# Fewer shift copies, an earlier first values product and split weight loads in a fused attention and MLP kernel

## The chip, the cores and the metric

The kernel runs on one core of a Trainium2 chip. The metric is the device time of one execution in microseconds. The version before takes 193.32 us (median of 6 runs, 193.03 to 193.96).

## The reference

The input x has 2048 positions of 448 values. Two blocks follow each other, each with a layer norm ahead of it and a residual around it.

```python
def _A_ref(x, wqkv, wo):            # 16 heads of 28
    qkv = x @ wqkv                  # -> q, k, v
    idx = pos[:, None] - 2 * arange(8)[None, :]        # 8 keys, two apart, masked where negative
    attn = softmax(where(mask, einsum(q, k[idx]) * scale, -1e9))
    return einsum(attn, v[idx]) @ wo

def _B_ref(x, w1, w2, w3, w4):      # F = 1792
    h = gelu(layernorm(x) @ w1)
    # four quarters of the 112 columns each, shifted by 1 down, 1 up, 2 down, 2 up along the positions
    hs = concatenate([g0, g1, g2, g3]) @ w2
    x1 = x + hs
    return x1 + gelu(layernorm(x1) @ w3) @ w4

h  = x + _A_ref(layernorm(x), A_wqkv, A_wo)
h2 = h + _B_ref(layernorm(h), B_w1, B_w2, B_w3, B_w4)
```

## The kernel before

**Chunks and tiles.** The 2048 positions are split into four chunks (c = 0 to 3) of 512. A chunk has four tiles of 128 positions. Its even positions are tiles 0 and 1 and its odd positions tiles 2 and 3, so that keys two positions apart stand side by side in one half. The 448 columns are laid out as four windows of 128 rows, which overlap, so that a matmul can use 64 rows of TensorE and two of them run at once.

**The stages of a chunk.** `phase_A1` computes the mean and variance of the four tiles, normalizes them into `lntm` and transposes them into `hT`. Chunks 0 and 1 are transposed by TensorE, with an evacuation from PSUM by `copy`, and chunks 2 and 3 by DMA. `phase_V` makes the values (`V_c`), five blocks of keys per half; `phase_QK` makes queries and keys (`QK_c.0` for heads 0 to 7, `QK_c.2` for heads 8 to 15). `phase_att` makes the scores of eight heads at a time (`S_c.g`, 80 small matmuls), the exponential on ScalarE, a mask on DVE, the products with the values (`AV_c.g`, 80 small matmuls) and the division by the sum (`N_c.g`). `phase_WO` is the output projection with the residual. `phase_B1` normalizes again, multiplies by w1 (`W1_c`), applies gelu, and makes the shifted copies (`G_c`). `phase_B2` multiplies by w2 (`W2_g`), `phase_W3` by w3 and `phase_B3` by w4 (`W4_g`). From w2 on the tiles are grouped anew, into groups of 2, 4, 4, 4 and 2 tiles, because a shift by two positions needs the neighbours' results.

**Quads.** `quad` (line 414) interleaves four products that go to two pairs of PSUM banks, T1 and T2. It makes four operations of TensorE: p1 and p2 start the products, p3 and p4 end those in T1 and T2. In `phase_V` p1 and p3 belong to the first two blocks of keys, which need only tiles 0 and 2, and p2 and p4 to the next two, which need all four tiles. A fifth product of values, `V_c.4`, follows.

**The first chunk.** `load0` issues the four tiles of x, then the weights: `win_load` (line 449) loads each of wqk and wv in two DMAs. `pad_wqk` (line 646) copies the query and key weights from `wqk_s` to `wqk_p` with 28 columns of a head padded to 32, by four copies of 128x896 elements (`pad`), and clears `wv_2`. For chunk 0 the square root is ScalarE's and the reciprocal DVE's (`inv_std_first`, line 565); later chunks take both from GpSimd.

**The shifts.** gelu of W1's second half goes to `gtm`. From there four copies of 32 partitions make `gB` and eight of 32 or 16 partitions make `gC`, each shifted by its own number of positions; in the last chunk three small memsets follow. `g_rows` (line 856) picks rows and offset for W2.

**What sets the order.** The code above only lists the operations and what each depends on. `_ORDER` (line 235) is a table of operation numbers, planned ahead of time: each engine executes its operations in the order of the table, a letter behind the number says which engine does a copy or a normalization (a: ScalarE, v: DVE, p: GpSimd), and the digits behind a colon name the PSUM banks. `_Sched.schedule` (line 159) reads it, `_emit_plan` (line 194) adds the waits. An engine never passes an operation that waits. The numbers `lat` and `occ` in the helpers served the planning and do nothing when the kernel runs. `WARM` is the number of TensorE's warm-up matmuls on zeros at the start, and `START` sets where TensorE's program begins within 256 instructions.

All instructions are recorded by one emitting line, so the profile has L1407 for all of them, and tiles and shapes tell them apart: `arena<-arena` is a pad, `ps<-arena,hT` values, `ps<-hT,arena` queries and keys, `ps<-qk` scores, `ps<-pt,vt` attention times values.

Of the kernel before, what the change touches and what calls it, by code (L numbers as in the profile page):

```python
# [228 lines left out]
WARM = 14  # L229
LATE = 2  # L230

START = 128
# [3 lines left out]
2 1 4 3 7 6 8 5 12 17 0 16 13 15 45 65 74 64 67 68 79 21 19 18:7 22 20 28 23 24 25 26 29 27 35 30 32 36:7 33:6  # L236
31 38 39:5 37a 41 34a 42:7 40v 43v 51:40 52 53 14 59 84 82 48v 156 47v 9 10 50a 62 63 80 49a 46a 78 69 134 132
72 73 138 136 135 139 133 137 11 178 142 54 180 85:62 71 86 87 88 184 205 185 140 182 70 179 98 99 101 103 102
113 109 111 110 106 107 104 112 108 105 57a 141 56a 97 89a 100 91:40 90a 92 220:26 93 201 181 143 221 223 144v
153v 150v 183 94 145:3 146a 147v 55:2 95a 96v 151:7 154:6 58v 148:3 152v 149v 203 76 75 77 222 224 188 155a  # L240
234:40 186 187 166:62 237 238 123p 167 168 204 60 235 236 61 225:54 198 165 115a 230 226 231 227 232 228 233 229
170a 169 171a 172:60 189 196a 173 174 175 197 239:54 161:3 240 244 241 245 242 246 243 247 66 130 190a 191 176a
177a 164a 346:06 382 192a 193 199 200 206 202 207 209 81 349 347 194v 157:42 158 159 117p 119v 160 348 208 162a
248:06 249 250 350 163a 360:24 252 251 361 254 253 210 213a 378:1 351:32 381a 363 362 255 356 260 364 256 121a
258 257 259 261 195 264 215a 389:60 352 390 214 118a 391 211a 217a 393a 262 365:54 370 366 371 367 372 368 369
218 263 392 394a 353 265 269v 267v 124 357 266a 383:26 354 535:04 538 373 536 219 384 385 386 355 388a 358 114p
268v 359 537 374:04 375 376 120v 387a 377 128 539 379a 116p 380a 528:26 416:04 529 417 270 418 531 419 540:6 530
216 532 126 420 421 403 424 122p 428 426 422 425 429 427 423 279:02 430 432 212 541a 543 125 431 280 281 282
533:6 283 534v 284 433 434v 437v 293a 294a 295a 439 436v 129 286v 288v 291v 292v 289v 440 404:04 435a 287a 405
406 407 296a 409a 542 408a 438 290a 273 271 272 274 544 441 395:62 396 397 398 285v 401v 400a 276v 278v 275v  # L250
277v 297:04 298 299 300 301 302 303 304 305 306 442 545 443a 549 446v 546 447:26 448 449 451 307 308 309 310 450
452 456v 459v 463v 454v 461a 457a 453v 462v 460a 458a 464a 445v 410:40 411 412 414a 455v 547 413 548 415v 131
312v 399:7 311v 402a 552 465:24 551 666:60 313 550 466 467 553 667 469 669 468 470 473 554:60 555 556 558 477
474 478 316:42 317 318 557 319 475 559 44 320 471 476 472 560 127 562 566 563 564 561 322:46 323 324 325 567 565
481 479 480 482 570 568 569 571 484v 579 483v 321 486v 328:02 577 578 314 329 330 331 327 326 334:46 335 670 332
336 333 668 338 337 485a 315 673:02 572v 340:5 487 339 343:7 676 574v 575a 573v 576 671:2 341 674 677 675 678:0
344 672v 489 490 492:64 493 494 488 495 491 680 679a 681 682 683 684 685 687 497 496 342 686 580 583v 585:02 586
587 588 589 590 599v 600a 595v 596v 592a 498:64 591v 594v 499 500 501 601a 593v 503 504:20 505 506 507 602a 597v
598v 581v 502 508 444v 603:64 604 605 607 83 609 611 509 610 688 510:02 511 512 513 689 612 606 608 691 613 514
615 690 616 614 515 617 516:7 519:6 692:42 693 694 695 517 520 618 518 619 620 623v 624v 621v 622a 625 627 521  # L260
697 696 704 698 700 701 699 705 702 703 706 707 708 525:7 744 522:6 629 745 526 523 709 713a 642:42 643 644 710v
712a 711v 524 714 717 626 527 645 584v 630:60 631 632 633 647 715 716 718 646 635 634 636:42 637 582v 638 640
746 639 641 723:60 724 725 648:24 649 650 727 652 726 728 722v 719v 732a 720v 736v 733v 735a 739v 730v 741a 734
731v 729v 742 738a 743a 740v 651 653 737 654:7 812:02 813 814 721v 815 655 816 817 820 345 818 821 819 749:64
750 751 752 824 753 754 757 656 755 758 822 823 825 756 759 761 762 760 765 747:3 628 663:2 763 764 660:7 826a
827a 828 664 766 748 661 662 770a 769v 768v 767v 657:6 849:24 850 851 852 771 658 831:60 832 833 854 853 835
837:24 834 836 838 839 840 843:06 844 845 842 841 829 846 848 830 847 782:24 783 784 788:06 786 785 787 789 790
791 792 793 665 776:42 777 778 780 794:60 795 796 797 779 781 799 858:5 659 774 806:4 855:3 859 856 857 860 798
772 775 800:7 807 773 801 802 808 803:6 809:7 804 805 810 811
# [3 lines left out]
def _fast_path(nc, es, flag, A_x, A_wqkv, A_wo, B_w1, B_w2, B_w3, B_w4, out):  # L273
# [33 lines left out]
    gB = sb("gB", [128, 2, HALF + 4], BF16)  # L307
    gC = sb("gC", [128, HALF + 4], BF16)
    gtm = sb("gtm", [128, 2, 768], BF16)
# [60 lines left out]
    def shift(out_ap, in_ap, n, on_pool=False):  # L370

        ka = dict(out=out_ap, in_=in_ap)
        op = S.add_many("flex", [("tensor_copy", ka)], 0, 0)
        op.opts = {"dve": [("tensor_copy", ka)], "pool": [("tensor_copy", ka)], "act": [("activation", dict(ka, func=ACT.Copy))]}
        op.lat = {"dve": dve_t(n, 3.0), "pool": 150 + n / 0.9, "act": 186 + n / 1.2}
        if not on_pool:
            del op.opts["pool"]
        op.occ = {e: v - {"dve": 82, "pool": 20, "act": 93}[e] for e, v in op.lat.items()}
        return op
# [34 lines left out]
    def quad(outs, lhsTs, rhss, n, T1, T2, blocks=(FIRST, SECOND) * 2):  # L414
# [20 lines left out]
        p1 = halves_op(series(0, 0, True), series(1, 1, True), g, mode)  # L435
        p2 = halves_op(series(2, 0, True), series(3, 1, True), (), mode)
# [12 lines left out]
    def win_load(name, dst, src, nbytes, engs):  # L449

        for k in range(2):
            dma("%s%d" % (name, k), dst[:, 2 * k:2 * k + 2, :],
                src[192 * k:192 * k + 256, :].rearrange("(c k) n -> k c n", k=128), nbytes / 2, engs[k],
                430.0)
# [4 lines left out]
    for il in range(4):  # L459
        dma("x0_%d" % il, xt(xin, 0, il, 1), x_rows(A_x, 0, il, 1), 128 * D * 2, ("sp", "act")[il % 2])  # L460
    win_load("wqk", wqk_s, A_wqkv[:, 0:2 * D], 512 * 2 * D * 2, ("sp", "sp"))
    win_load("wv", wv_s, A_wqkv[:, 2 * D:3 * D], 512 * D * 2, ("sp", "sp"))
# [17 lines left out]
    def init1():  # L480
# [28 lines left out]
        pool("memset", 140, ap=gB[:, :, 0:2], constant=0.0)  # L509
        pool("memset", 140, ap=gB[:, :, HALF:HALF + 2], constant=0.0)  # L510
        pool("memset", 140, ap=gC[:, 0:2], constant=0.0)

    def load_attn_out():
# [9 lines left out]
        for g in range(4):  # L523
            for h in range(2):
                k = 64 * h + 32 * (g // 2) + 16 * (1 - g % 2)
                dma("w2%d" % (3 + 2 * g + h), w2_s[k:k + 16, 3, :], w2v[96:112, g, :], 16 * D * 2)
# [4 lines left out]
        for x in range(2):  # L531
            for g, o in ((x, 384), (2 + x, 480), (2 + x, 544), (x, 576)):
                o += 16 * (1 - x)
# [31 lines left out]
    def inv_std_first(i0):  # L565
# [933 lines left out]
```

## Time and profile before

| | us |
|---|---|
| median of the runs | 193.32 |
| the profiled execution | 192.8 |
| its span | 191.1 |
| TensorE busy with matmuls | 182.9 |
| DVE busy | 128.8 |
| ScalarE busy | 112.2 |
| GpSimd busy | 41.2 |
| first matmul that isn't warm-up | 6.61 |
| last matmul ends | 188.24 |

The profile records one execution, whose own time stands beside its span; the difference lies before the first and behind the last instruction. PE is TensorE's matmuls, PEld its weight loads, DVE the vector engine, ACT ScalarE, POOL GpSimd, SP the engine that issues most DMAs. In a timeline the first number is the start in us, the second the duration, and a bracket gives the idle time ahead of it and what ended it; consecutive instructions of one kind are one line with a count. In the groups, busy time and mean duration in ns stand ahead of the second bar.

### The profile page before, as it was taken

How to read it: one execution, taken by the hardware profiler on the slowest of the kernel's cores; microseconds unless marked ns; L12 is line 12 of the kernel's file. 1: busy time of each engine (PE TensorE's matmuls, PEld its weight loads, DVE VectorE, ACT ScalarE, POOL GpSimd, SP SyncE). 2: the span in 40 equal slices, each digit the busy share in tenths (PEclk: the TensorE clock that was granted, in tenths of full speed). 3: DMA queues.
4: the chain of work that ended last, by engine and by line, in shares of the span. 5: the costliest groups of instructions: out<-in, count | busy, mean ns of one | idle time of the engine just before them, and what ended most of it. 6: DMA issues, size and time to landing. Idle time of an engine off the chain costs nothing.

```text
span 191.1 us, 6790 instructions
## 1 busy us (share of the span) xinstructions
PE 182.9 (96%) x2999; PEld 102.5 (54%) x2999; DVE 128.8 (67%) x313; ACT 112.2 (59%) x149; POOL 41.2 (22%) x101
## 2 busy tenths in 40 slices
PE   7899999997998998999999999999999999999994
PEld 2455556553556573577556464444566568455551
DVE  7799998999986689999773379894038970001241
ACT  2869899597849849938658920117691326554000
POOL 4137500607104603006900002042000320000000
PEclk9999999999999999999999999999999999999999
DMA  5965316427397766730643600507000233000031
GB/s 139 336 225 157 81 36 146 34 33 137 106 171 201 196 157 139 47 113 3 123 107 95 159 3 2 141 18 182 0 0 27 47 98 98 3 0 3 3 100 51
DMA packets 32479, 17.77 MB, mean 93 GB/s; under 512 B 22524, under 2 KB 31932, under 8 KB 32444
## 3 DMA queue, kind: packets, MB, share of 16 engines
q1 hardware_dynamic: 32156, 17.05, 38.5%
q8 instruction: 25, 0.41, 0.9%
q10 hardware_dynamic: 288, 0.23, 0.4%
q14 instruction: 10, 0.08, 0.2%
HBM read 10.07 MB, written 1.90 MB: 63 GB/s over the span
## 4 chain that ended last, share of the span: by engine, by line
PE 74%; DVE 10%; ACT 8%; DMA 3%; SPq 1%; issue 1%
PE ps L1407 74%; DVE st L1407 4%; DMA arena<-in_A_wqkv_dram 3%; ACT gC L1407 2%; DVE osb L1407 1%; ACT gtm L1407 1%; SPq L1407 1%; DVE xin L1407 1%; ACT gA L1407 1%; ACT pt L1407 1%; ACT vt L1407 1%; DVE arena L1407 1%; ACT arena L1407 1%; DVE lntm L1407 1%; DVE pt L1407 1%
## 5 line engine op out<-in xcount | busy, mean ns | idle before, releaser
L1407 PE MATMUL ps<-actT,w_s 64*128 64x512 bf16 (+2 forms) x560 | 44.2, 312 | 0.0
L1407 PE MATMUL ps<-w_s,arena 128*128 128x448 bf16 x224 | 43.4, 353 | 0.1
L1407 DVE TENSOR_TENSOR xb<-ps,xb 128x448 bf16<-128x448 f32 (+1 forms) x26 | 18.4, 723 | 32.8 <-PE ps L1407 32.7
L1407 ACT ACTIVATE arena<-ps 128x512 bf16<-128x512 f32 (+2 forms) x40 | 29.0, 767 | 16.9 <-PE ps L1407 16.6
L1407 PEld LDWEIGHTS ps<-actT,w_s 64*128 64x128 bf16 x560 | 26.4, 94 | 16.9 <-DVE xb L1407 0.4
L1407 PEld LDWEIGHTS ps<-w_s,arena 128*128 128x128 bf16 x224 | 21.4, 98 | 21.0 <-issue 0.6
L1407 PE MATMUL ps<-hT,arena 64*128 64x512 bf16 x224 | 25.9, 377 | 0.2
L1407 POOL TENSOR_TENSOR rstd<-vtmp,mhalf 128x4 f32<-128x4 f32 (+1 forms) x16 | 18.1, 1133 | 1.1
L1407 DVE BATCH_NORM_STATS2 st<-xin 128x6 f32<-128x448 bf16 x32 | 18.1, 604 | 0.2 <-DMA xin<-in_A_x_dram 0.2
L1407 ACT ACTIVATE pt<-ps 128x1024 bf16<-128x1024 f32 x16 | 15.7, 1022 | 3.7 <-PE ps L1407 3.6
L1407 PEld LDWEIGHTS ps<-hT,arena 64*128 64x128 bf16 x224 | 10.7, 94 | 11.9 <-ACT qk L1407 0.5
L1407 ACT ACTIVATE lntm<-xin,nmr,rstd 128x512 bf16<-128x512 bf16 x13 | 10.2, 808 | 9.0 <-POOL nmr L1407 8.3
L1407 PE MATMUL ps<-arena,hT 64*64 64x448 bf16 (+1 forms) x248 | 15.1, 352 | 0.2 <-DVE hT L1407 0.2
L1407 ACT ACTIVATE qk<-ps 128x1024 bf16<-128x1024 f32 x14 | 13.9, 1021 | 2.1 <-PE ps L1407 2.0
L1407 POOL TENSOR_SCALAR nmr<-mv 128x4 f32<-128x4 f32 (+1 forms) x16 | 5.1, 319 | 42.5 <-DVE mv L1407 42.3
L1407 POOL TENSOR_SCALAR vtmp<-mv 128x4 f32<-128x4 f32 (+1 forms) x16 | 3.4, 213 | 49.5 <-DVE mv L1407 48.6
L1407 PE MATMUL ps<-wo_s,oT 64*128 64x448 bf16 x128 | 13.1, 350 | 0.5 <-ACT vt L1407 0.5
L1407 PE MATMUL ps<-actT,w_p 64*128 64x512 bf16 (+1 forms) x140 | 13.0, 333 | 0.0
L1407 ACT ACTIVATE lntm<-xb,nmr,rstd 128x512 bf16<-128x512 bf16 x5 | 4.0, 811 | 15.1 <-POOL nmr L1407 15.1
L1407 DVE COPY gC<-gtm 32x256 bf16<-32x256 bf16 (+1 forms) x15 | 3.3, 220 | 13.6 <-ACT gtm L1407 13.2
L1407 DVE TENSOR_TENSOR pt<-pt,msk 128x1024 bf16<-128x1024 bf16 x16 | 10.5, 679 | 1.0 <-ACT pt L1407 1.0
L1407 PEld LDWEIGHTS ps<-arena,hT 64*64 64x64 bf16 (+1 forms) x248 | 7.6, 107 | 5.6 <-ACT gC L1407 0.8
(90 smaller groups left out, 226.5 us busy)
## 6 DMA issues: line engine op xcount, KB each, us to landing
w_s<-in_B_w_dram SPq DMA_DIRECT2D x6, 448.0 KB, 4.4
rzb<-rz_scratch SPq DMA_DIRECT2D x8, 256.0 KB, 4.6
out_dram<-xb SPq DMA_DIRECT2D x16, 112.0 KB, 2.2
xin<-in_A_x_dram SPq DMA_DIRECT2D x3, 448.0 KB, 7.3
arena<-in_A_wqkv_dram SPq DMA_DIRECT2D x2, 448.0 KB, 5.8
w_s<-in_B_w_dram SPq DMA_DIRECT2D x2, 336.0 KB, 5.1
arena<-in_A_wqkv_dram SPq DMA_DIRECT2D x2, 224.0 KB, 5.1
w_s<-in_B_w_dram SPq DMA_DIRECT2D x2, 224.0 KB, 2.9
```

The lines of the kernel that those rows point to most:

```text
L1407: inst = getattr(eng, meth)(**kw)
```

## The change

Five things change, and a new order table goes with them.

1. **Shift copies.** `gB`, `gC` and `gtm` become one tensor `gBC` of four planes. gelu writes its three parts straight into planes 0 to 2. Partitions whose shift is zero need no copy in planes 0 and 1; the others are shifted in place by two copies, and plane 3 is made from plane 2 by five. That is seven copies a chunk, with no memset in the last chunk. The rows of w1's and w2's last window are arranged anew to match.
2. **First values.** In chunk 0 only tiles 0 and 2 are transposed ahead of the values. Then come p1, the transposes of tiles 3 and 1, p3, p2, the fifth product and p4. In the new table queries and keys of heads 0 to 7 stand between p2 and the fifth product.
3. **Weight loads.** wv is loaded first, then wqk in eight DMAs: by half of the heads, by pair of windows, and by query and key. Two of the eight are issued by ScalarE. The four pads follow the halves: two for heads 0 to 7, two for heads 8 to 15.
4. **Sums by ScalarE.** For tile 3, ScalarE takes the sum and the sum of squares in two activations with an accumulated output; DVE takes the statistics of the other three. All four tiles are normalized by DVE.
5. **Planning numbers** for activations and DMAs change, and with them the table: engines, banks and order of nearly all operations. In the table DVE's memset of `wo_s` stands ahead of the first statistics.

```diff
-WARM = 14
+WARM = 11
-START = 128
+START = 134
...
+        if mids:
+            mid = mids[0]()
+            p3 = halves_op(series(1, 0, False), series(0, 1, False), (), mode)
+            p2 = halves_op(series(2, 0, True), series(3, 1, True), (), mode)
+            last = mids[1]()
+            p4 = halves_op(series(3, 0, False), series(2, 1, False), (), mode)
...
+            chain([p3, p2, last, p4])
+            return
...
-    for il in range(4):
-        dma("x0_%d" % il, xt(xin, 0, il, 1), x_rows(A_x, 0, il, 1), 128 * D * 2, ("sp", "act")[il % 2])
-    win_load("wqk", wqk_s, A_wqkv[:, 0:2 * D], 512 * 2 * D * 2, ("sp", "sp"))
-    win_load("wv", wv_s, A_wqkv[:, 2 * D:3 * D], 512 * D * 2, ("sp", "sp"))
+    for k, il in enumerate((0, 3, 2, 1)):
+        dma("x0_%d" % il, xt(xin, 0, il, 1), x_rows(A_x, 0, il, 1), 128 * D * 2, ("sp", "act")[k % 2], bw=450.0)
+    win_load("wv", wv_s, A_wqkv[:, 2 * D:3 * D], 512 * D * 2, ("sp", "sp"), 190.0)
+    for h in range(2):
+        for k in range(2):
+            for e in range(2):
+                o = D * e + D // 2 * h
+                dma("wqk%d%d%d" % (h, k, e), wqk_s[:, 2 * k:2 * k + 2, o:o + D // 2],
...
+                    "act" if e > h else "sp", 430.0, 280.0)
...
+    def first_norm():
+
+        m_, v, r_ = mv[:, 0], vtmp[:, 0], rstd[:, 0]
+        x, y = xin[:, 3, :], xb[:, 3, :]
+        act(y, x, ACT.Identity, 448, scale=-1.0 / 448, accum_out=m_[:, 3, 0:1])
+        act(y, x, ACT.Square, 448, bias=m_[:, 3, 0:1], accum_out=m_[:, 3, 1:2])
+        for i in (0, 2):
+            ln_stats(0, xin[:, i, :], i)
+        inv_std_first(slice(0, 4, 2), 2)
+        ln_stats(0, xin[:, 1, :], 1)
+        inv_std_first(slice(1, 2), 1)
+        act(v[:, 3:4], m_[:, 3, 1:2], ACT.Sqrt, 1, bias=epsb[:], scale=1.0 / 448)
+        dve("reciprocal", 160, out=r_[:, 3:4], in_=v[:, 3:4])
+        for i in (0, 2, 3, 1):
+            dve("tensor_scalar", 390, out=lntm[:, 0, i, :, :], in0=windows(xin[:, i, :]), scalar1=m_[:, i, 0:1], scalar2=r_[:, i:i + 1],
+                op0=ALU.subtract if i < 3 else ALU.add, op1=ALU.mult)
...
-        for w in range(4):
-            copy(wqk_p[:, w, :, 0:28], wqk_s[:, w, :].rearrange("p (j d) -> p j d", d=28), 896, psum=False, mode=3.0)
+        for h in range(2):
+            for k in range(2):
+                copy(wqk_p[:, 2 * k:2 * k + 2, :, 0:28].rearrange("p w (e j) d -> p (w e) j d", e=2)[:, :, 8 * h:8 * h + 8, :],
+                     wqk_s[:, 2 * k:2 * k + 2, :].rearrange("p w (e j d) -> p (w e) j d", e=2, d=28)[:, :, 8 * h:8 * h + 8, :],
+                     896, psum=False, mode=3.0)
...
-        gt = gtm[:, c % 2, :]
-        act(gt, T2(lambda p: p.rearrange("k u n -> k (u n)")[:, 0:768]), ACT.Gelu_apprx_tanh, 768)
+        o = 2 + 256 * c
+        act(gBC[:, 0:3, o:o + 256], T2(lambda p: p.rearrange("k u n -> k (u n)")[:, 0:768].rearrange("k (t n) -> k t n", t=3)),
+            ACT.Gelu_apprx_tanh, 768)
         tag("G_%d" % c)
-        for q, sh in enumerate((0, -1, 0, -2)):
-            r = slice(32 * q, 32 * q + 32)
-            o = 2 + 256 * c + sh
-            shift(gB[r, :, o:o + 256], gt[r, 0:512].rearrange("k (p n) -> k p n", p=2), 512)
-        for q, (s1, s2) in enumerate(((-1, 0), (-1, 1), (0, 1), (-1, 1))):
-            for m, sh in ((32, s2), (16, s1)):
-                r = slice(32 * q, 32 * q + m)
-                o = 1 + 256 * c + sh
-                shift(gC[r, o:o + 256], gt[r, 512:768], 256)
-                if c == NCH - 1 and m == 32 and s1 < 0:
-                    dve("memset", 145, ap=gC[32 * q:32 * q + 16, HALF:HALF + 1], constant=0.0)
+        last = c == NCH - 1
+        for r0, m, d, e in ((32, 32, 1, 1), (96, 32, 2, 2)):
+            v = gBC[r0:r0 + m, 0:2, :]
+            shift(v[:, :, o - d:o - d + 256 + e * last], v[:, :, o:o + 256 + e * last], 512)
+        for r0, m, d, e in ((0, 128, 0, 0), (0, 32, 2, 1), (32, 16, 1, 0), (96, 32, 1, 0), (96, 16, 2, 1)):
+            v = gBC[r0:r0 + m, :, :]
+            shift(v[:, 3, o - d:o - d + 256 + e * last], v[:, 2, o:o + 256 + e * last], 256)
```

The order of some stretches, read from the new table with the operations' names:

```
TensorE: warm-up, transposes of tiles 2, 0, V_0 p1, transposes of tiles 3, 1, V_0 p3, V_0 p2, QK_0.0 p1 to p4, V_0.4, V_0 p4,
         QK_0.2 p1, S_0.0, QK_0.2 p2, p3, transposes of chunk 1, QK_0.2 p4, QK_1.0 p1, p2, S_0.1, QK_1.0 p3, p4, AV_0.0, QK_1.2, AV_0.1,
         V_1.4, S_1.0, V_1, S_1.1, WO_0 p1 to p3, AV_1.0, WO_0 p4, QK_2.2 p1 to p3, AV_1.1, QK_2.2 p4, QK_2.0 p1 to p3, S_2.1,
         QK_2.0 p4, V_2.4, S_2.0, V_2, WO_1 p1 to p3, AV_2.0, AV_2.1, WO_1 p4, W1_0, V_3, QK_3.0 p1, p2, W2_0, QK_3.0 p3, p4,
         W1_1, QK_3.2, W2_1, S_3.0, V_3.4, W3_0.0, WO_2, ...
DVE:     memsets (zz, msk, ident, mt, mhalf, eps, wqk_p, w1_p, wo_s), statistics of tiles 0, 2, reciprocal, normalize 2, 0,
         statistics of tile 1, evacuate tile 0, reciprocals of 3 and 1, normalize 3, 1, memset wv_2, a pad of heads 0 to 7,
         evacuate tile 1, the other pad of heads 0 to 7, ...
ScalarE: four DMAs, square root of 0 and 2, the two sums of tile 3, evacuate tile 2, square roots of 3 and of 1, evacuate tile 3, ...
SP:      ..., DMA transposes of chunk 2 in the order 1, 2, 3, 0, ...
```

## The prediction

> **What bounds the kernel now.** I read the page first (busy shares, slices, chain), then the start in order of time, then TensorE's own timeline for its idle places, then the groups by shape.
>
> ```profile
> PE 182.9 (96%) x2999; PEld 102.5 (54%) x2999; DVE 128.8 (67%) x313; ACT 112.2 (59%) x149; POOL 41.2 (22%) x101
> PE   7899999997998998999999999999999999999994
> PEclk9999999999999999999999999999999999999999
> PE 74%; DVE 10%; ACT 8%; DMA 3%; SPq 1%; issue 1%
> q8 instruction: 25, 0.41, 0.9%
> ```
>
> TensorE is the bound: 96% busy at full granted clock. The change removes no useful matmul, so only TensorE's idle time can move. The start:
>
> ```profile
> 2.92 0.48 DVE L1407 MEMSET w_p<- 128x512 uint32 x1
> 3.56 1.15 DVE L1407 BATCH_NORM_STATS2 st<-xin 128x6 f32<-128x448 bf16 x2 [0.15 <-DMA xin<-in_A_x_dram]
> 6.61 0.62 PE L1407 MATMUL ps<-ident,lntm 128*128 128x128 bf16 x8
> 8.43 2.84 PE L1407 MATMUL ps<-arena,hT 64*64 64x448 bf16 x56 [0.22 <-DVE hT L1407]
> 9.40 1.47 DVE L1407 COPY arena<-arena 128x896 bf16<-128x896 bf16 x2 [0.70 <-DMA arena<-in_A_wqkv_dram]
> 11.00 0.81 DVE L1407 MEMSET wo_s<- 128x896 uint32 x1
> 11.21 4.92 PE L1407 MATMUL ps<-hT,arena 64*128 64x512 bf16 x44
> ```
>
> Four values products (56 matmuls) start at 8.43, and queries and keys follow at 11.21 without a hole: the padded weights are ready at 10.87. Later TensorE stands still mainly here:
>
> ```profile
> 44.54 0.78 PE L1407 MATMUL ps<-qk 28*64 28x52 bf16 x75
> 46.19 0.22 PE L1407 MATMUL ps<-qk 28*64 28x51 bf16 x5 [0.87 <-issue]
> 52.72 3.20 PE L1407 MATMUL ps<-wo_s,oT 64*128 64x448 bf16 x32 [0.45 <-ACT vt L1407]
> 61.11 0.21 PE L1407 MATMUL ps<-pt,vt 64*32 64x51 bf16 x5 [0.55 <-issue]
> 76.33 0.55 PE L1407 MATMUL ps<-w_s,gA 64*128 64x448 bf16 x4 [0.52 <-ACT qk L1407]
> 143.78 0.37 PE L1407 MATMUL ps<-w_s,gA 64*128 64x224 bf16 x4 [0.33 <-ACT gC L1407]
> ```
>
> From 80 to 140 TensorE is busy 59.83 of 60 us, so nothing can be won there. Two of these waits are behind ScalarE's shift copies:
>
> ```profile
> L1407 ACT ACTIVATE gC<-gtm 16x256 bf16<-16x256 bf16 x11 | 4.6, 414 | 0.5 <-DVE gC L1407 0.3
> L1407 ACT ACTIVATE gC<-gtm 32x256 bf16<-32x256 bf16 x6 | 2.5, 414 | 0.2
> L1407 ACT ACTIVATE gB<-gtm 32x512 bf16<-32x512 bf16 x3 | 1.9, 629 | 0.1
> L1407 DVE COPY gB<-gtm 32x512 bf16<-32x512 bf16 x13 | 3.6, 280 | 0.4
> L1407 DVE COPY gC<-gtm 32x256 bf16<-32x256 bf16 x10 | 2.2, 221 | 13.4 <-ACT gtm L1407 13.2
> ```
>
> **What the Trainium skill says.** "Runtime: NRT & Kernel Launch", section "Instruction fetch mechanics": an engine's instructions come in blocks of 16 KiB, 256 of them, fetched while the block before runs. The trace agrees: 25 packets make 0.41 MB, and the two "issue" waits lie 383 matmuls apart, 766 instructions with their weight loads, about three blocks; both fall inside the dense groups of 80 small matmuls. "TensorE: Matmul & The Clock Gate", Part 1: TensorE runs at half rate until some 3.4 us of activity. The trace agrees: warm-up matmuls start 0.43 us apart until 5.49, then faster.
>
> **The change, part by part.**
>
> *Start.* DVE's memsets ahead of the first statistics gain wo_s (0.81 plus a 0.05 gap) and mhalf (0.06), and lose the one of wv_2 (0.30 with its gap): statistics begin near 4.0 to 4.1 instead of 3.56. Two statistics and two aggregates took 1.37, square root, reciprocal and two normalizations about 1.4 (durations of the same rows): first transposes near 6.45, against 6.61. ScalarE's two sums of tile 3 aren't in the trace; a 128x448 activation with operands took 0.74, so 0.65 to 0.85 each; I take 0.75. They stand behind the square root (5.7) and ahead of ScalarE's evacuation, which ends near 7.7. First values then at 7.85: 0.6 earlier. But now the square roots of tiles 3 and 1, two reciprocals and two normalizations are left (9.2), then on DVE, in this order, the wv_2 memset (0.3), a pad of half the heads (0.67), tile 1's evacuation (0.4) and the second pad (0.75). The second half of the values waits for the evacuation (10.5), queries and keys for the pad: 11.25. At that point 12 matmuls of the values (12 x 0.0495 = 0.60) are still owed. **+0.65**. Two of the eight weight loads are issued by ScalarE, 0.43 each as its other two, ahead of its table load (1.28), which ends at 3.85 instead of 2.99, with the square root not due before 5.5: hidden. Their rows of 448 bytes aren't in the trace. A packet of 1792 bytes took 75 ns on its DMA engine and one of 896 took 41; so the first halves' 1024 packets on 16 engines take between 1.2 us (by bytes, as before: no extra) and 2.6 (41 ns each: +1.4). The pads come at 9.4 and 10.4, while as many bytes as are needed by then, 1.38 MB, had landed by 7.2 in the trace: hidden at both ends, and I take 0. x1, which on SP now goes ahead of the second halves, lands near 10.7 as before, and they by 12.5, for pads at 12.5 and 14. If that cover went, each us would be paid whole. Three matmuls of warm-up fewer cost nothing: TensorE waits for data anyway. If the clock came on late, each us of the first products at half rate would cost 0.5; their pauses are under 1 us. START + 6 makes up for their 6 instructions, so the block borders stay where they are in the code behind.
>
> *To 40 us.* I lay the new order out with the old durations. The first scores wait for a bank that values' second evacuation frees (0.25), transposes of chunk 1 for an exponential (0.2), the products after them for an evacuation (0.3); before had 0.27 and small ones: lag **0.76** at 21.3. One bank wait for a DVE evacuation at 26: **0.95** at 31. Behind AV_0.1 DVE then has, from 30.15, four stream transposes to oT and two from PSUM (0.63 each from start to start), two scalings (0.58), two reciprocals (0.3) and a normalization (0.33), 5.6 us, so the output projection starts at 35.8, not before: +0.55. The DMA transpose of tile 3 of chunk 2 waits for that normalization (34.5), and tile 0's is queued behind it on SP although ready at 24: it starts near 36.5 and at about 4 us lands near 40.4: +0.65. Before's own small waits there give back 0.3: **1.85** behind at QK_2.2, from 1.1 to 2.7.
>
> *40 to 62 us.* Before needs 22.14 us (39.32 to 61.46) for 19.0 us of matmuls: 3.15 lost, 1.42 of it instruction fetch. The new order spreads the dense groups; it loses some 0.95 where S_2.0 waits for queries and keys that ScalarE evacuates behind an exponential, 0.4 for the DMA transpose of chunk 0, 0.25 for banks and fetch: **0.3** behind.
>
> *62 to 80 us.* Shift copies fall from 12 to 7 per chunk. By the order lists ScalarE does 6 instead of 20 of them: from 11 x 0.44 + 6 x 0.44 + 3 x 0.63 = 9.4 us (0.44 from start to start) to about 2.8; DVE 22 instead of 28 and 3 memsets fewer. This is worth only what TensorE waited: after W1_1 ScalarE now has two gelus and two copies, 2.85 us, under the 3.1 us of QK_3.2, and W2_1 uses banks that QK_3.2 doesn't. The waits at 76.3 and 80 and the fetch and bank waits near 61 go: about -1.05, **-0.75**.
>
> *After 140 us.* The last chunk's copies had TensorE wait 0.33, 0.45 by starts; two W4 tiles now stand between. -0.45. Elsewhere the order is close to the old one but had no wait to lose: I add +0.45 for new waits that I haven't followed: **-0.75** in all.
>
> The profiled execution took 192.8 with a span of 191.1; it becomes 192.05 and 190.35. The median of the runs stands 0.5 above: 193.3 - 0.75 = **192.6**.
>
> **Rivals.** *Fetch goes too* (191.3): no block border between 21 and 62 costs TensorE anything, 1.42 less than before instead of about equal. For it: the shortest block was 2.6 us of matmuls (ending at 46.19) and is now 3.3. Against: five blocks lie under 3.8 us, and the two waits in the trace ended 4.0 and 4.8 us after the border before. *A wash* (193.3): the shift copies' gain of 1.5 is eaten by waits at banks between 80 and 188, where the trace has none to win. *Slower* (194.2): the late DMA transpose of chunk 2. In the trace such a transpose took 2.5 to 5.0 us from issue to landing, and one queued directly behind another was held up at issue 2.5 us. If QK_2.2 begins at 41.5 or later, 1.1 more than in my sum, the change loses more than it wins; at 42 it gives 194.2. Against it: other loads are fewer by then. *The early values do nothing* is part of my forecast: they come 0.6 earlier and the queries don't.
>
> **How the numbers follow.** Forecast 0.50, fetch gone 0.10, wash 0.14, late transposes 0.26. A measurement of this kernel tells about 0.2% (0.39 us) from no change, so faster is below 192.9 and slower above 193.7: 0.60, 0.14, 0.26. The forecast's own range is 191.9 to 193.0. For 8 in 10 it reaches to the fetch case (191.2) and the late transposes (194.3), which also holds the unknown sums on ScalarE (0.2 either way) and the packets (up to +1.3, not likely to be uncovered).
>
> **What would show it.** First V matmuls at 7.6 to 8.1; then holes, and QK_0.0 near 11.25; statistics from 4.0. WO_0 and QK_2.2 waiting on DVE and DMA, TensorE 1 to 2.5 us behind at 40. No ScalarE wait ahead of W2_1, none at the last chunk's W2. Wrong it is if QK_0.0 starts before 10.8 or after 11.8, if "issue" waits of TensorE sum outside 0.5 to 2.2 us, or if waits of over 1 us appear beyond 80.

## The result: no difference that can be measured

| | before | after |
|---|---|---|
| median, us | 193.12 (71 executions) | 193.48 (34 executions) |
| lowest to highest | 192.19 to 194.11 | 191.34 to 196.57 |
| standard deviation | 0.40 | 1.24 |
| profiled execution / its span | 192.8 / 191.08 | 195.61 / 193.77 |

The ratio of the times is 0.9993, 95% interval 0.998 to 1.0006. The comparison behind this ratio leaves out executions over 1.5% above a kernel's fastest, and the changed kernel has many of them, so its median of all executions stands 0.36 us above. The profiled execution happens to be a long one. A second one of the same kernel (below, the first experiment) took 193.07 with a span of 191.34, and both are read here.

The page of the changed kernel, first profile: busy shares, TensorE's slices, and the chain that ended last. The granted clock is full in every slice and the 25 packets of instructions are those of before.

```profile
PE 183.2 (95%) x2996; PEld 102.6 (53%) x2996; DVE 124.1 (64%) x302; ACT 107.8 (56%) x141; POOL 37.9 (20%) x99
PE   7899998999799999999999999999999999999992
PE 89%; ACT 4%; DVE 3%; issue 2%
```

DVE has 4.7 us less to do and ScalarE 4.4 us, and TensorE doesn't end sooner: it was the bound and has the same matmuls but for three of the warm-up. The start, from the timelines of TensorE and DVE (start, duration, idle time ahead in brackets):

```profile
4.04 1.09 DVE L1447 BATCH_NORM_STATS2 st<-xin 128x6 f32<-128x448 bf16 x2
6.38 0.72 PE L1447 MATMUL ps<-ident,lntm 128*128 128x128 bf16 x8 [0.25 <-DVE lntm L1447]
7.66 0.95 PE L1447 MATMUL ps<-arena,hT 64*64 64x448 bf16 x16 [0.56 <-DVE mv L1447]
8.96 0.33 DVE L1447 COPY arena<-arena 128x896 bf16<-128x896 bf16 x1
9.64 0.38 DVE L1447 COPY arena<-arena 128x896 bf16<-128x896 bf16 x1
10.75 2.55 PE L1447 MATMUL ps<-hT,arena 64*128 64x512 bf16 x22
```

The values start at 7.66 instead of 8.43, queries and keys at 10.75 instead of 11.21. From 7.66 on there is no hole. But 12 matmuls of the values, 0.60 us, are still owed at 10.75, so TensorE stands 0.14 behind, not 0.46 ahead. TensorE's idle places from 15 us on, first profile:

```profile
32.16 0.66 PE L1447 MATMUL ps<-qk 28*64 28x51 bf16 x60 [0.69 <-issue]
...
49.11 0.24 PE L1447 MATMUL ps<-qk 28*64 28x51 bf16 x11 [0.88 <-issue]
51.42 0.83 PE L1447 MATMUL ps<-qk 28*64 28x52 bf16 x80 [0.44 <-ACT qk L1447]
63.01 0.61 PE L1447 MATMUL ps<-actT,w_p 64*128 64x256 bf16 x6 [0.47 <-issue]
81.68 1.71 PE L1447 MATMUL ps<-actT,w_s 64*128 64x256 bf16 x28 [0.43 <-issue]
101.82 3.21 PE L1447 MATMUL ps<-actT,w_p 64*128 64x512 bf16 x35 [0.42 <-ACT arena L1447]
```

The waits of before at 76.3 and 143.8, behind shift copies, are gone. New are 0.43 at W3_0.0 (81.68) and 0.42 at W1_2 (101.82). The profile names no releaser for the first of them, but it is a wait for a PSUM bank. In the new table W3_0.0 writes a bank that holds scores of S_3.0 until ScalarE's exponential has read them:

```profile
80.44 1.02 ACT L1447 ACTIVATE pt<-ps 128x1024 bf16<-128x1024 f32 x1 [0.58 <-PE ps L1447]
```

This exponential ends 0.21 us ahead of W3_0.0 in all ten profiles of the new order, and the wait is 0.43 in all ten. The DMA transpose of W3_0.0's input isn't what it waits for, though two profiles name it: it landed between 0.37 and 1.14 ahead of the product, and the wait is the same. W1_2 starts 0.14 behind the landing of its DMA transpose in all nine profiles with these block borders, whatever the line names, so it waits for that. The other waits for "issue" are 3.15 us together, against 1.43 before. The shift copies by shape:

```profile
L1447 DVE COPY gBC<-gBC 32x512 bf16<-32x512 bf16 x6 | 1.7, 286 | 0.7 <-ACT gBC L1447 0.7
...
L1447 ACT ACTIVATE gBC<-gBC 16x256 bf16<-16x256 bf16 x3 | 1.2, 414 | 0.1
```

ScalarE has six of them left in all, DVE 22, as the order said. Last the end, from SyncE's and DVE's timelines. The first line is a group of four stores that ends at 191.40:

```profile
185.44 5.96 SPq L1447 DMA_DIRECT2D out_dram<-xb  x4
...
190.09 0.62 DVE L1447 TENSOR_TENSOR xb<-ps,xb 128x448 bf16<-128x448 f32 x1 [0.81 <-PE ps L1447]
```

The last store was issued at 191.07, 0.36 us after the last addition had ended, and landed 2.20 later. Before, it followed the addition by 0.03 and landed after 1.66. From TensorE's last matmul to the end of the span it is 2.85 us before and 3.73 after.

**Where the time went.** I cut TensorE's program into its operations (a part of a quad, one group of scores). From the time between an operation's start and the next one's I subtracted the least that it took in any of seven profiles of both orders. The sum of what is left is time lost, warm-up included (the ledger). "Issue" waits other than W3_0.0's are taken out and stand in a line of their own.

| after the same share of TensorE's work, about | before | after, first | after, second | second minus before | forecast |
|---|---|---|---|---|---|
| 17 us | 7.21 | 7.78 | 7.69 | +0.48 | +0.65 |
| 22 us | 7.60 | 8.09 | 7.94 | +0.34 | +0.76 |
| 33 us | 7.90 | 8.59 | 8.43 | +0.53 | +0.95 |
| 43 us | 8.09 | 9.05 | 9.01 | +0.92 | +1.85 |
| 66 us | 9.69 | 10.06 | 10.06 | +0.37 | +0.3 |
| 87 us | 10.66 | 10.65 | 10.65 | -0.01 | -0.75 |
| 107 us | 10.96 | 11.44 | 11.55 | +0.59 | |
| TensorE's end | 11.98 | 12.09 | 12.20 | +0.22 | -0.75 |
| "issue" waits | 1.43 | 3.15 | 0.61 | -0.82 | about 0 |
| behind TensorE's end | 2.85 | 3.73 | 3.72 | +0.87 | 0 |

From the row at 66 us on, the forecast isn't quite the same thing as the other columns: it has the 1.42 us of "issue" waits of before in it, which those leave out. The last three rows add up: +0.11, +1.72 and +0.88 make 2.71 for the first profile, whose span is 2.69 longer than before; +0.22, -0.82 and +0.87 make 0.27 for the second, 0.26 longer. The forecast of 0.75 fell in three places: waits for data and for a bank between 66 and 107 us, the end, and the waits for instructions, which scatter.

### The profile page after: what moved, and what is told of

Its sections match the earlier page's. It is cut to its first block, busy times and chain, and to the rows that moved or that the text cites. A ratio compares the mean times of both kernels' runs of the same rounds, so it can differ in the third digit from the quotient of the medians.

```text
span 193.8 us, 6769 instructions
## 1 busy us (share of the span) xinstructions
PE 183.2 (95%) x2996; PEld 102.6 (53%) x2996; DVE 124.1 (64%) x302; ACT 107.8 (56%) x141; POOL 37.9 (20%) x99
## 4 chain that ended last, share of the span: by engine, by line
PE 89%; ACT 4%; DVE 3%; issue 2%
PE ps L1447 89%; ACT vt L1447 1%; ACT pt L1447 1%; DVE st L1447 1%; ACT arena L1447 1%; ACT qk L1447 0%; DVE wo_s L1447 0%; DVE lntm L1447 0%; DVE xb L1447 0%; DVE w_p L1447 0%; DVE rzb L1447 0%; DVE msk L1447 0%; DVE hT L1447 0%; DVE mv L1447 0%; ACT vtmp L1447 0%
## 5 line engine op out<-in xcount | busy, mean ns | idle before, releaser
L1447 PE MATMUL ps<-hT,arena 64*128 64x512 bf16 x224 | 26.5, 377 | 0.3 <-issue 0.2
L1447 POOL TENSOR_SCALAR vtmp<-mv 128x4 f32<-128x4 f32 (+1 forms) x16 | 4.5, 280 | 90.6 <-DVE mv L1447 90.1
L1447 POOL TENSOR_TENSOR rstd<-vtmp,mhalf 128x4 f32<-128x4 f32 (+1 forms) x16 | 16.7, 1041 | 0.8
L1447 DVE COPY gBC<-gBC 32x256 bf16<-32x256 bf16 (+4 forms) x22 | 5.1, 246 | 12.0 <-ACT gBC L1447 11.5
L1447 PEld LDWEIGHTS ps<-actT,w_p 64*128 64x128 bf16 x140 | 8.4, 94 | 5.7 <-issue 1.5
L1447 DVE TENSOR_SCALAR lntm<-xin,mv,rstd 128x512 bf16<-128x512 bf16 x24 | 8.8, 402 | 2.8 <-POOL nmr L1447 2.8
```

The costliest lines, as they stand in the source:

```text
L1447: inst = getattr(eng, meth)(**kw)
```

## The experiments

"Run 1" and so on are the experiments by number, "kernel 4" is the kernel of the fourth.

My theory after the result: the shift copies give what was forecast where they stand, but DMA transposes and weight chains give it back; the start gains nothing; and which block of instructions comes late differs from execution to execution. Rivals: the shift copies were never on the path; the early values do harm; the clock falls.

**1. The changed kernel again**, nothing edited.

> The changed kernel as it is, for a second profile. Fetch theory: its time is set by instruction-fetch waits of TensorE at the borders of its 256-instruction blocks; the data waits stay within 0.3 us of the first profile (about 1.9 us after 11 us), and the sum of the issue waits differs from 3.5 us by as much as the profiled execution's time differs from the first one's. Data theory: the issue waits stay near 3.5 us whatever the time, and the data waits carry the difference.

Measured: median 193.38 against 192.78, ratio 1.001 (0.9983 to 1.0037). TensorE's waits in its profile, those at 26.83 (0.19), 36.11 (0.50), 49.58 (0.43) and 50.59 (0.18) left out:

```profile
31.41 0.66 PE L1447 MATMUL ps<-qk 28*64 28x51 bf16 x60 [0.42 <-issue]
...
79.19 1.71 PE L1447 MATMUL ps<-actT,w_s 64*128 64x256 bf16 x28 [0.43 <-issue]
99.39 3.21 PE L1447 MATMUL ps<-actT,w_p 64*128 64x512 bf16 x35 [0.49 <-ACT arena L1447]
```

The two executions of one program differ by 2.54 us in time, and the sum of their "issue" waits (3.58 and 1.04) differs by 2.54. The wait of 0.88 in the scores at 49.11 isn't there at all. So a single profile can't settle a change of this size.

**2. Borders of blocks moved, after.** No instruction changes; TensorE's program starts 128 instructions, half a block, elsewhere.

```diff
-START = 134
+START = 6
```

> START 6 in place of 134: every block border moves by 128 instructions, no operation moves. Fetch theory: blocks of 1.1 to 2.7 us of matmuls appear where before the shortest is 3.6, so at about 4.2 us of latency per block 5 to 8 us are added: 198 to 202 us, all of it in issue waits at the new borders. Data theory: within 0.5 us of the changed kernel.

Measured: 202.02, ratio 1.049 (1.0448 to 1.0532), +8.6 us on the changed kernel. The longest of its "issue" waits (the next one is 1.14 at 35.19), and two stretches with TensorE's busy time and, third from the end, the granted clock:

```profile
62.87 0.29 PE L1447 MATMUL ps<-pt,vt 64*32 64x51 bf16 x26 [2.31 <-issue]
...
8.81:12.22 3.41, 3.23 (x32) 0.50 1.13 305
63.42:66.83 3.41, 3.41 (x22) 0.50 0.44 117
```

The profiled span is 7.9 us longer than that of run 1. Some 3.8 of this are "issue" waits (4.87 against 1.04). Some 3.3 are these two stretches, in which TensorE was busy at half rate; the second lies right behind the wait of 2.31. The mean clock was 0.975 to 0.987 in all four executions, and in no execution of the changed kernel below 0.991. Another 1.3 is a late start: the last two tiles of x landed 1.8 us later than in run 1 (5.80 and 6.03 instead of 4.05 and 4.24), which held the first transposes up to 7.71. The rest, waits that came or went and a shorter end, gives back some 0.5. Why x was late isn't shown, so not all of the 8.6 is shown to come from the borders; but the "issue" waits alone grew by more than the whole change was to gain.

The waits do follow the borders. Counted in TensorE's instruction records, every "issue" wait of over 0.15 us lies at place 126 or 127 of 256 in the profiles of the changed kernel, and here at 254 or 255, the 128 places of the edit. W3_0.0's wait alone stays where it was, at 223. The Trainium skill ("Runtime: NRT & Kernel Launch", section "Instruction fetch mechanics") calls the cost of a border "mostly hidden"; here it isn't, and the measurement decides.

**3. Borders moved, before.**

```diff
-START = 128
+START = 0
```

> The kernel before with its TensorE program moved by half a block (START 0 instead of 128), not one instruction changed. Theory (instruction fetch is a cost of every order of this program, and where the borders fall sets it): with the borders at START 0 the shortest stretches between two borders are 1.2, 2.25 and 2.9 us, against 3.1, 3.6 and 3.6 in the kernel before. In the changed kernel the same move made shortfalls below 4.2 us of 10.6 instead of 2.5 and cost 8.6 us; here they are 7.1 instead of 2.7, so +4.5 us, from 3.5 to 5.5: near 197.5, as waits for nothing that the profile shows, at the borders. Rival (only the changed kernel's order is open to it): within 0.3 us of the kernel before.

The edit doesn't do what the expectation says. With `START = 0` the kernel leaves the alignment out (`if reg is not None and START`), and the program begins where it happens to. Before, the two waits lie at places 132 and 133 of 256, here the three longest at 193 and 194: the borders moved by some 60 instructions and not by 128.

Measured: 194.05 against 192.89, ratio 1.0058 (1.0036 to 1.0081): +1.1 us, not the +4.5 expected.

```profile
50.46 2.64 PE L1407 MATMUL ps<-arena,hT 64*64 64x448 bf16 x49 [1.32 <-issue]
```

With those of 0.65 at 31.62, 0.34 at 54.20 and smaller ones it makes 2.54 against 1.43, 1.1 more. In this profile two other things about cancel: the queries came 0.43 later, behind a warm-up whose rate came on at 7.24 and not at 5.41, and the wait of 0.45 ahead of WO_1 is gone. So the old order pays for fetch too. My measure of it, how far a block's matmuls fall short of 4.2 us (an estimate), isn't tested here, since its +4.4 was worked out for other borders. In run 2 it said +8.1, and the "issue" waits grew by 3.8: the sign came, the size didn't, and that 8.6 came in all is luck.

**4. The seven shift copies alone, on the kernel before.** `gBC`, the copies and the rows of w1 and w2 are those of the change; the order is the old one without the copies that fall away (17 on DVE, 11 on ScalarE are left).

```diff
-    gB = sb("gB", [128, 2, HALF + 4], BF16)
-    gC = sb("gC", [128, HALF + 4], BF16)
-    gtm = sb("gtm", [128, 2, 768], BF16)
+    gBC = sb("gBC", [128, 4, HALF + 4], BF16)
...
-        for q, sh in enumerate((0, -1, 0, -2)):
...
+        for r0, m, d, e in ((32, 32, 1, 1), (96, 32, 2, 2)):
...
+        for r0, m, d, e in ((0, 128, 0, 0), (0, 32, 2, 1), (32, 16, 1, 0), (96, 32, 1, 0), (96, 16, 2, 1)):
```

> The kernel before with the seven shift copies alone: its own order, the five copies of plane 3 put where five of its eight gC copies were, with their engines (11 copies on ScalarE instead of 20, 17 on DVE). Predicted mechanism: the waits at 76.3 (0.52) and 143.8 (0.33, 0.45 by starts) go: 0.5 to 1.0 us faster. Rival: the order around W2 doesn't use it and the waits stay: within 0.2 us.

Measured: 192.59 against 192.78, ratio 0.9985 (0.9959 to 1.0011): from 0.8 us faster to 0.2 slower, so neither the forecast nor its rival is excluded by the time. Its waits:

```profile
56.17 3.21 PE L1400 MATMUL ps<-actT,w_p 64*128 64x512 bf16 x35 [0.32 <-DMA actT<-lntm]
...
98.95 3.21 PE L1400 MATMUL ps<-actT,w_p 64*128 64x512 bf16 x35 [0.26 <-DMA actT<-lntm]
```

The waits at 76.3 (0.52) and 143.8 (0.33) are gone, as the forecast said. In their place it waits for DMA transposes at 56.17, 60.66 (0.31) and 98.95, where the kernel before didn't wait, and for an exponential at 78.90 (0.27 instead of 0.07). In the ledger it loses 0.82 between 87 and 107 us, where the kernel before loses 0.30. So the copies were on the path, at 0.85 us, and in this profile most of that is given back to the next event that keeps its own time. This execution had no "issue" wait at all. A kernel held up by fetch may hide waits for data: in the profile of run 5, with 1.37 us of "issue" waits, those for these three DMA transposes are 0.23, 0.13 and 0.30.

**5. GpSimd's work away from the pads**, on kernel 4.

```diff
 GpSimd: memsets and selects of msk, qk, gBC
-GpSimd: copy of 128x64 in hT, which waits until 8.7
 GpSimd: memsets of vt and gA, four selects
+GpSimd: copy of 128x64 in hT
```

> The kernel before with the seven shift copies, and GpSimd's copy of 128x64 put behind its memsets and selects of the start, which then run at 4 to 7.5 us and no longer beside DVE's two pads. Theory (the pads took 0.65 to 0.80 because GpSimd was working beside them): the same pads, in the old form of one window and all heads, take 0.33 to 0.40 us each. Rival (the form by halves of the heads is what is faster): they still take 0.65 to 0.80. In time nothing either way, since TensorE is busy with values until 11.2: within 0.2 us of the kernel with the seven copies alone (0.9985 of the time before); if GpSimd's work now slows DVE's first statistics, up to 0.5 us more.

Measured: 192.8 against 192.89, ratio 0.9992 (0.9975 to 1.0009). Its two pads on DVE, and GpSimd beside the pads in the kernel before:

```profile
9.31 0.69 DVE L1400 COPY arena<-arena 128x896 bf16<-128x896 bf16 x2 [0.62 <-DMA arena<-in_A_wqkv_dram]
```

```profile
8.92 0.96 POOL L1407 MEMSET vt<- 128x240 bf16 x2
...
9.59 1.03 POOL L1407 TENSOR_SCALAR_AFFINE_SELECT msk<-msk 128x408 bf16<-128x408 bf16 x1
```

The pads of the old form take 0.394 and 0.386 once GpSimd is quiet, against 0.752 and 0.796 beside it. GpSimd is held up too: the select of 408 took 1.03 beside the pads and 0.72 here. So the form by halves of the heads is not what made the pads short. The Trainium skill ("GPSIMD Engine Reference", section "Specifications") says that GpSimd shares its SBUF interfaces with VectorE and contends with VectorE instructions in a 2-port performance mode or with two inputs in SBUF. These runs show the contention, 0.75 to 0.80 us against 0.39; which mode the copies ran in they don't tell.

**6. The early values undone.** Transposes of tiles 3 and 1 ahead of the first values.

```diff
 TensorE: transposes of tiles 2, 0
-TensorE: V_0 p1
 TensorE: transposes of tiles 3, 1
+TensorE: V_0 p1
```

> The changed kernel with the transposes of tiles 3 and 1 put back ahead of the first values product; nothing else moved. Theory: in the changed kernel TensorE has no hole between the first values (7.66) and the queries (10.75), so with the values held up until all tiles are normalized (DVE ends them at 8.81) the values begin near 9.3, the queries near 11.4 to 11.5, and TensorE is 0.6 to 0.8 us behind from there; the end is 0.4 to 0.8 later than the changed kernel's, about 193.9 to 194.2 where the changed kernel has 193.4. My prediction's own statement (the early values do nothing because the queries wait for the pads) gives a start of the queries within 0.2 of 10.75 and no difference.

Measured: 195.42 against 192.89, ratio 1.0093 (1.0054 to 1.0132). Values start at 9.26 as expected, queries at 13.18 and not at 11.4 to 11.5. The busy times of TensorE, its weight loads, DVE, ScalarE and GpSimd in the window from 9.2 to 12.5, and behind them the granted clock, 0.50:

```profile
9.20:12.50 3.30, 3.23 (x34) 1.28 (x36) 3.20 (x9) 0.45 (x2) 1.51 (x6) 0.50 1.12 310
```

Behind a wait of 1.44 us TensorE ran 3.3 us at half rate; from 12.5 to 15 the clock is 1.00. In 6 of 12 executions the mean clock was 0.982 to 0.991. That mixes two things, so:

**7 and 8. Warm-up of 14 again**, in the changed kernel and in kernel 6.

```diff
-WARM = 11
+WARM = 14
-START = 134
+START = 128
```

> The changed kernel with 14 warm-up matmuls again instead of 11, and START 128, which keeps the borders where they are. The warm-up then ends near 6.5 instead of 5.9 to 6.1, so the first transposes come 0 to 0.25 us later (6.38 to 6.6), and the first values, which wait for tile 0's evacuation and for wv (landed 7.26), stay at 7.66 to 7.8. Theory (three warm-up matmuls fewer are what lets TensorE's rate fall in 3 of 56 executions of the changed kernel and of its variant with the late memset, with a mean granted clock near 0.99 and 1.5 to 3 us more): no execution below 0.995 among some 20, median within 0.3 us of the changed kernel's 193.4, highest execution below 196. Rival (the warm-up's length has nothing to do with it): one or more low ones, the same median.

> The changed kernel with the transposes of tiles 3 and 1 ahead of the first values (as in the run before) and 14 warm-up matmuls, START 128. With 11 of them, 6 of 12 executions had a mean granted clock of 0.982 to 0.991, and in the profiled one TensorE's first three quarters of the values ran at half rate (groups of four 64x448 matmuls 0.374 us apart from 9.26 to 12.2, then 0.187) behind a wait of 1.44 us. Theory A (the length of the warm-up decides whether the rate holds through that wait): no or hardly any low clocks, median 194.0 to 194.5. Theory B (the wait itself lets the rate fall): still about half of the executions low, median 195 to 195.5. In both the values begin near 9.3 and, at full rate, the queries near 11.6.

Measured beside each other: 193.35 (ratio 1.0011, 0.9986 to 1.0035) and 194.81 (1.0064, 1.0041 to 1.0086). A mean clock below 0.995 came in 1 of 17 and in 2 of 20 executions. For the changed kernel the length of the warm-up makes no difference that shows; for kernel 6 the low clocks are rarer with 14 but not gone, and 2 of 20 against 6 of 12 leaves open how much is the warm-up's. With the rate full, kernel 6's queries start at 11.93, 1.18 later than in the changed kernel, and it takes 1.0 us (ratios) to 1.5 us (medians) longer. In kernel 7's profile the rate came on late: transposes at 7.12, values at 8.30, queries at 11.39, 0.64 later than in the changed kernel. Its span is only 0.18 longer than that of run 1, since it had 3.10 us behind TensorE's end and not 3.72.

**9. The memset of `wo_s` later.**

```diff
-DVE: memset of wo_s ahead of the first statistics
+DVE: memset of wo_s behind the second pad of heads 0 to 7
```

> The changed kernel with DVE's memset of wo_s moved from ahead of the first statistics to behind the second pad of heads 0 to 7. If the start is TensorE's bound as predicted: statistics from about 3.6 instead of 4.04, first queries and keys about 0.45 earlier (10.3 instead of 10.75), and the kernel 0.3 to 0.5 us faster. Fetch theory: the first 0.45 shows at QK_0.0, but most of it is given back at block borders by 64 us, and the median gains 0.2 at most.

Measured: 192.88 against 192.78, ratio 0.9985 (0.9965 to 1.0006).

```profile
5.86 0.72 PE L1448 MATMUL ps<-ident,lntm 128*128 128x128 bf16 x8 [0.24 <-DVE lntm L1448]
7.98 0.95 PE L1448 MATMUL ps<-arena,hT 64*64 64x448 bf16 x16 [1.40 <-DVE lntm L1448]
```

The transposes come 0.52 earlier and the values don't: DVE and ScalarE have the columns ready by 7.1, but the second half of wv lands at 7.74 in this execution (7.26 in the first of the changed kernel). The queries start at 10.98, 0.23 later than in the changed kernel and not 0.45 earlier. At the start the weights are next in line behind DVE.

**10. The last two DMA transposes of chunk 3 later.**

```diff
-SP: DMA transposes of A1_3.3, A1_3.2; loads of w2; DMA transpose of B1_0; load of w2; stores of the sums zp
+SP: loads of w2; DMA transpose of B1_0; DMA transposes of A1_3.3, A1_3.2; load of w2; stores of the sums zp
```

> The changed kernel with the last two DMA transposes of chunk 3 put behind that of the first tile of phase_B1 on SP, so that they run at 57 to 62 us instead of 43.5 to 49.3. Theory (the fetch of TensorE's instructions is late where DMA transposes overlap: the packet at 45.57 took 2.27 us between three of them, and TensorE waited 0.88 at 49.11 in one run, 0.51 at 48.09 in another, nothing in a third): no wait at the border near 48 to 49, other borders as before, median 0.2 to 0.5 us below the changed kernel's, so 193.0, and fewer runs above 194.5. Rival (fetch is late for its own reasons, whatever the transposes do): the same waits and the same median within 0.2.

Measured: 195.65 against 192.89, ratio 1.0118 (1.006 to 1.0175), over 6 executions. In the profile the "issue" waits fall to 0.13, and a wait of 1.84 stands at W2_0:

```profile
63.93 0.55 DVE L1448 RECIPROCAL rzp<-zp 128x64 f32<-128x64 f32 x1 [3.91 <-DMA zp<-osb]
...
66.96 0.37 PE L1448 MATMUL ps<-w_s,gA 64*128 64x224 bf16 x4 [1.84 <-ACT gBC L1448]
```

I had moved two transposes past the loads of w2, and with them ahead of the stores of `zp`. DVE's reciprocal waits for those, the shift copies are queued behind it on DVE, ScalarE's copy behind DVE's, and W2_0 behind that. The theory that these transposes delay the fetch isn't shown: one quiet profile is within the scatter. What makes a fetch late stays open.

**11. Another order of the last tiles.** In the changed kernel the last store has a wait for the landing of the one before, as the second of a pair of tiles; in the kernel before, the pairs are apart.

```diff
-W4_3.2, W4_3.3, W4_3.0, W4_3.1, and their additions and stores
+W4_3.2, W4_3.0, W4_3.3, W4_3.1
```

> The changed kernel with the last W4 tiles in another order: W4_3.2, 3.0, 3.3, 3.1 instead of 3.2, 3.3, 3.0, 3.1, and their additions and stores with them. Theory: in the changed kernel the last two stores are a pair, and the last one has a wait for the landing of the one before it (in three profiles it was issued 0.06 to 0.07 us after that landing, 0.25 to 0.36 after the last addition, and landed 2.2 to 2.3 later; before, issue followed by 0.03 and landing by 1.66). With the other tile between them no store waits: the time from TensorE's end to the end of the span falls from 2.85 to 3.73 (3.35 as a mean over eight profiles of the changed kernel and its variants) to 2.85 to 2.9, and the median by 0.3 to 0.6 us, to 192.9 to 193.1. Rival (the landing is long for another reason): stretch behind TensorE's end still 3.1 to 3.7 in this profile, median 193.4.

Measured: 192.99 against 193.0, ratio 0.9992 (0.9971 to 1.0012). The stretch behind TensorE's end is 2.99 (3.35 as a mean of eight profiles with the other end). In time that is 0.4 below run 1's median, with an interval that holds no difference. The last store is issued at 188.51, 0.03 after the last addition, and the group of two ends at 188.84:

```profile
186.91 1.93 SPq L1448 DMA_DIRECT2D out_dram<-xb  x2
187.86 0.62 DVE L1448 TENSOR_TENSOR xb<-ps,xb 128x448 bf16<-128x448 f32 x1 [0.97 <-PE ps L1448]
```

**12. Both 9 and 11.**

> The same end, and in addition the memset of wo_s behind the second pad of heads 0 to 7. If both gains add up (0.3 to 0.6 from the end; 0.3 to 0.5 from the memset, as measured by the medians 192.88 and 193.4), 192.4 to 192.6, 0.1 to 0.3% below the kernel before. Rival: the memset's difference was the scatter of the changed kernel (its executions reach from 191.3 to 196.6), and the median is that of the run beside it.

Measured: **192.26 against 193.0**, ratio 0.9966 (0.9946 to 0.9985), the only one of these kernels whose interval lies below 1: 0.3% faster than the kernel before, and by the medians 1.1 us faster than the changed one. Its profiled execution, 193.87, had 2.60 us of "issue" waits and 2.88 us behind TensorE's end, so it isn't shown that the two edits do this and nothing else; the sum of their single medians (0.4 and 0.5) is about what came.

## Why the prediction was right or wrong

The time lies in the range of 191.2 to 194.3, but not where I put it. My likeliest case, faster at 192.6, did not come; "a wash" did, to which I gave 0.14. The range held because it was wide enough for no change, and because errors of both signs met: up to 43 us the sum was 0.9 too slow, from 66 to 87 it was 0.7 too fast. That is luck.

- **Start, +0.65.** Right in sign, measured +0.14 by starts and +0.48 in the ledger. Statistics at 4.04 (4.0 to 4.1), transposes at 6.38 (6.45) and values at 7.66 (7.85) hold, ScalarE's sums too (0.56 and 0.67, and an accumulator read of 0.18 each that I didn't know of: 0.74 and 0.85 for my 0.75). The step that failed is the pads at 0.67 and 0.75: I took the row of before, without looking at who else worked at that time. Alone they take 0.33 to 0.39 (run 5). That put the queries at 10.75, below my own bound of 10.8.
- **"The early values do nothing".** Wrong as a statement about the new order: without them the queries come 1.18 later and the kernel takes 1.0 to 1.5 us more (run 8). They make up for tiles 3 and 1, which the new start normalizes later.
- **Weight loads at nothing.** Right for the pads: the halves for heads 0 to 7 landed by 8.15, the pads came at 8.96. I didn't see that wv's own landing is next in line behind the early values (run 9).
- **To 40 us, 1.85 behind.** Measured 0.92. The wait of S_2.0 behind ScalarE and the wait ahead of WO_0 came, 0.44 and 0.50 in size, but WO_0's is put down to an evacuation of the values by ScalarE, not to DVE's chain; and QK_2.2 waited for no DMA transpose. The term of 0.65 for it was wrong, and so is the *Slower* rival.
- **62 to 80 us, -1.05.** The term that failed most: -0.38 from 66 to 87 in the ledger. The wait of 0.52 went, and 0.43 came at W3_0.0 for the bank of S_3.0's scores. I had looked at W2_1's banks and not at those of the product after it: I had named what goes and not what is late next. The *wash* rival, waits at banks between 80 and 188, had this one right, and a DMA transpose (0.42 to 0.49 at W1_2) made the rest.
- **The sum and the fetch.** The text says fetch about equal, and the sum doesn't keep to it. From 40 to 62 us it sets the 3.15 us lost before, 1.42 of them fetch, against 1.6 in the new order, with 0.25 "for banks and fetch": nearly all of the fetch is gone there. The 0.55 at 61.11 lies in that stretch and goes once more "near 61" in the next. With fetch kept equal, the same terms make about +0.7 instead of -0.75, a slower kernel. The *fetch goes too* case takes the 1.42 off a second time.
- **After 140, -0.45.** Right: from 107 us to the end the second profile gains 0.37. **New waits, +0.45.** Right in size (+0.60 from 87 to 107) by luck, since it stood for waits that I hadn't followed.
- **The end.** I followed the last wait of TensorE and took what lies behind it as before. The new order puts a pair of stores last: +0.87 in both profiles, 0.50 as a mean over eight (3.35 - 2.85). A forecast has to go on to the last store.
- **Fetch about equal.** Over nine profiles of the new order with these borders the "issue" waits without W3_0.0's are 0.13 to 3.15, mean 1.25; over three of the old order 0 to 1.43, mean 0.93. Equal within their scatter, but 3.58 in the first profile lay outside my 0.5 to 2.2. The bound was too narrow, and the blocks that pay differ between executions. The shortest block before, which I put at 2.6 us, is about 3.0 us long.

The sum, from the means: 0.22 at TensorE's end, 0.32 of fetch and 0.50 behind it make +1.0 in profiles, where the medians of all executions say +0.36 to +0.60; the ratio says 0.

## What to carry to other kernels

When a wait goes, find the next event that keeps its own time (here DMA transposes, an exponential that holds a PSUM bank, a chain of sums through DRAM, the landing of weights) and count only the distance to it. Take a duration from a row only after looking at what the engine that shares its path did at that time. In a sum of gains, count each wait once, and take off only what the forecast says will go. And follow a new order to the last store.

## What the runs showed of the hardware

- TensorE's instruction fetch decides more than most edits here: with the block borders moved, the waits at them grew by 3.8 us in one order (by 128 instructions) and by 1.1 in another (by some 60), and two executions of one program differed by 2.54 us in these waits alone.
- A DVE copy of 128x896 took 0.33 to 0.39 us with GpSimd quiet, 0.75 to 0.80 beside it.
- An activation with an accumulated output is followed by an instruction of its own, 0.18 to 0.19 us.
- A wait of 1.44 us, with 0.7 us of transposes ahead of it, was enough for TensorE to fall to half rate for 3.4 us in some executions of a program and not in others. Behind a wait of 2.31 us it fell too, again for 3.41 us.
